# A cached-attention and ReGLU decode block: the last K loaded between two halves of a V, the last V but one as moving operand, and the W_o sets laid out anew

## The chip, the core and the metric

The kernel runs on one core of a Trainium2 chip. The core has a matrix engine (TensorE, PE in the profile; its weight loads are shown as PEld), a vector engine (VectorE, DVE), a scalar engine (ScalarE, ACT), GpSimd (POOL) and SyncE (SP), which here issues nearly all the transfers. The engines run on their own and wait for one another at semaphores. Sixteen DMA engines carry the data between the chip's memory (HBM) and the on-chip memory (SBUF); matmul results land in PSUM. The metric is the device time of one execution in microseconds (us), median of the runs; lower is better.

## The reference

Two sequences (B = 2), one new token each. Layer norm, attention over a cache of 8192 keys and values for 32 heads of width 128, output projection, residual; then layer norm, a gated MLP with a ReLU gate (F = 1376), residual. All tensors are bf16.

```python
D = 512; Hq = Hkv = 32; Sk = 8192; Dh = 128; F = 1376
q = (layernorm(x) @ wq)                       # per head
scores = einsum("bhqd,bhkd->bhqk", q, k_cache) * Dh ** -0.5
p = softmax(scores)
h = x + einsum("bhqk,bhkd->bhqd", p, v_cache) @ wo
n = layernorm(h)
gate = n @ W_gate; up = n @ W_up
out = h + (relu(gate) * up) @ W_down
```

K and V together are 268 MB of the 281 MB that are read: every key and every value is used once.

## The kernel before

**Steps.** One step handles one pair of heads of one sequence: N = 32 steps, numbered i = 0 to 31 (i // 16 is the sequence). K and V of a step are 4 MB each. `kbuf` and `vbuf` have two slots, used by i % 2. Each partition holds NT = 128 tokens of 128 numbers; partitions 0 to 63 belong to the one head, 64 to 127 to the other.

**Scores.** The work on K is shared. TensorE takes the last NPE = 32 of the 128 tokens of each partition (`scores_pe`, lines 287 to 330: 128x128 transposes at L311, ScalarE copies them out of PSUM at L313, a matmul with q at L302, small transposes back at L321). VectorE takes the first 96: `products` (L338) multiplies K in place by a replicated q, `scores` (L353, L357) adds up the 128 numbers of each token by halving. In the last step the split is 48 to 80 (`NPE_LAST`, `share`). `largest` (L368) spreads the maximum, `exponentials` (L380, L383) writes the weights to `pgz`, which also has two slots, and the sums to `zc`.

**Values.** `values(i, part)` (lines 390 to 415) holds 8 columns of `pgz` as stationary operand and streams V as the moving one: 32 matmuls of 512 columns, 16 in each half. ScalarE copies the result out (L406), and once per group of steps `o_ps` is picked from its diagonal blocks (L411, 8 small fp32 matmuls). `values_cols` (lines 417 to 426) turns this round: each 128x128 block of V is loaded as the stationary operand and multiplied by two columns, 128 weight loads and 128 matmuls, and the result needs no picking. The steps before the last two use `values`; i = 30 and i = 31 use `values_cols`.

**Output projection.** W_o is 4 MB. Where many rows of W_o are contiguous in HBM, several heads are treated as a set: `SETS` lists (first head, heads, partitions, place), `spread` (L437, L442) and `attend_set` (L456, L459, L461, L464) rearrange the head outputs to the layout that the set's rows have in SBUF. The heads from `HM` on are done one by one by `attend` (L472). A set is done when its heads are ready in the second sequence (`behind`).

**Order.** The program is written out by hand (`manual_schedule`): every engine runs its instructions in the order of the code. SP issues the loads in program order too, each when its buffer's last readers are done. The last loads are issued in this order: K 30 (584.2 us), V 29 (589.6), K 31 (604.1), V 30 (610.2), the four pieces of V 31 (623.3 to 630.2), W_gate, W_up and three pieces of W_down. W_gate and W_up go to slot 0 of `kbuf`, W_down to `wd_sb`. Up to eight transfers of this queue are on the way at once: each takes one of eight semaphores in turn.

**The end.** After the last step come the sums, `values_cols(31)`, the last heads' `attend`, the second layer norm (lines 541 to 552), gate and up (L561), and down (L588), whose last two chunks are those that are loaded last.

Of the kernel before, what the change touches and what calls it, by code (L numbers as in the profile page):

```python
# [7 lines left out]
ACT = mybir.ActivationFunctionType  # L8
# [15 lines left out]
def kernel(  # L24
# [13 lines left out]
    nc = tc.nc  # L38
# [5 lines left out]
    KC = D // P  # L44
# [6 lines left out]
    NPE = NT // 4  # L51
    NPE_LAST = 3 * NT // 8
    TPC = 8
# [12 lines left out]

    SETS = [(0, 16, P, 0), (16, 8, P, 16), (24, 3, 48, 32)]
    WO_T = 24
    HM = 27

    assert Sq == 1 and Hkv == Hq and Dh == P and D == KC * P and Hq == 32 and NPE % TPC == NPE_LAST % TPC == 0
    assert F == 11 * P - AGAIN
# [39 lines left out]

    QZ = 2 * NPE_LAST // 4
    qz = consts.tile([P, B, NG, 2 * QZ], bf16)
# [6 lines left out]

    def load_kv(cache, buf, i, pieces=1):
        b, g = steps[i]
        w = ROW // pieces
        for k in range(pieces):
            nc.sync.dma_start(
                out=buf[:, i % 2, k * w:(k + 1) * w],
                in_=_dram(cache, (b * Hkv + 2 * g) * Sk * Dh + k * w, [[ROW, P], [1, w]]),
            )
# [19 lines left out]
    with tc.manual_schedule():  # L149

        xr = wd_sb[0:B, 0, :]
        nc.scalar.dma_start(out=xr, in_=_dram(A_x, 0, [[D, B], [1, D]]))
# [19 lines left out]
        nc.gpsimd.memset(qz, 0.0)  # L172
        nc.gpsimd.memset(wbig[0:HALF, SETS[2][3] * D:(SETS[2][3] + SROWS[2]) * D], 0.0)
        nc.gpsimd.memset(placed, 0.0)
# [44 lines left out]

        for (h0, n, w, at), r in zip(SETS, SROWS):  # L220
            part, rows = (P, [[r * D, P]]) if w == P else (24, [[r * D, 6], [6 * r * D, 4]])
            for k in range(w // part):
                nc.sync.dma_start(
                    out=wbig[32 * k:32 * k + part, at * D:(at + r) * D],
                    in_=_dram(A_wo, (h0 * Dh + part * k * r) * D, rows + [[1, r * D]]),
                )
# [54 lines left out]

        def share(i):

            npe = NPE_LAST if i == N - 1 else NPE
            return NT - npe, npe

        def scores_pe(i):
            b, g = steps[i]
            s = i % 2
            kt = kbuf[:, s, :]  # L290
            nv, npe = share(i)


            U = npe // 4
# [12 lines left out]
            for c0 in range(0, npe, TPC):  # L307
                t_ps = ps2.tile([P, TPC, P], bf16, tag="tp")
                for k in range(TPC):
                    t = nv + c0 + k  # L310
                    nc.tensor.transpose(t_ps[:, k, :], kt[:, t * Dh:(t + 1) * Dh], ident)  # L311
                kTs[c0] = small.tile([P, TPC * P], bf16, tag="kT", name="kT", bufs=2)
                nc.scalar.activation(out=kTs[c0], in_=t_ps.rearrange("p t s -> p (t s)"), func=ACT.Copy)  # L313
                if c0:
                    times_q(c0 - TPC)
            times_q(npe - TPC)
# [7 lines left out]
            scol = small.tile([P, NT], f32, tag="scol")  # L324
            scols[i] = scol
            for j in range(2):
                r = slice(j * HALF, (j + 1) * HALF)
                nc.scalar.activation(  # L328
                    out=scol[r, nv:NT].rearrange("p (u t) -> p t u", t=4), in_=sc_ps[r, :, :, j], func=ACT.Copy,
                )  # L330

        def products(i):

            b, g = steps[i]
            kt = kbuf[:, i % 2, :]
            nv, _ = share(i)
# [7 lines left out]
        def scores(i):  # L344

            kt = kbuf[:, i % 2, :]
            scol = scols[i]
            nv, _ = share(i)
            width = Dh
# [40 lines left out]
        def values(i, part):  # L390
# [12 lines left out]
            if part == 0:  # L403
                return
            w = (g // 4) % 2
            nc.scalar.activation(out=pv[r, w], in_=pv_ps[i][r, :], func=ACT.Copy)  # L406
            if i in groups:
                first, n = groups[i][1:]
                o_ps[i] = ps.tile([P, 8], f32, tag="of", name="o_ps")
                for t in range(VG):  # L410
# [19 lines left out]
        def spread(k):  # L430

            h0, n, w, at = SETS[k]
            nq = Dh // SROWS[k]
            sps = []
            for b in range(B):
# [5 lines left out]
                if w != P:  # L441
                    nc.vector.tensor_copy(  # L442
                        _free(placed, b * HALF, [[32, 2], [1, 4], [4, 6]]), _free(sp, 0, [[24, 2], [6, 4], [1, 6]]),
                    )
                    sp = placed[:, b, :]
                sps.append(sp)
            return sps

        def attend_set(k, sps, last=False):

            h0, n, w, at = SETS[k]
            r = SROWS[k]
            p1 = P if w == P else HALF
            or_ps = ps.tile([P, B, r], f32, tag="mx")
            for b in range(B):
                nc.tensor.matmul(out=or_ps[0:p1, b, :], lhsT=sps[b], rhs=rest[k], start=True, stop=True)  # L456
            o, i = orow[k][0:p1], or_ps[0:p1].rearrange("p b c -> p c b")
            if last:
                nc.vector.tensor_copy(o, i)  # L459
            else:  # L460
                nc.scalar.activation(out=o, in_=i, func=ACT.Copy)  # L461
            for c0 in range(r):
                for c in range(KC):
                    nc.tensor.matmul(  # L464
                        out=att_ps[:, c, :],
                        lhsT=_free(wbig[0:p1], (at + c0) * D + c, [[KC, P]]), rhs=orow[k][0:p1, c0, :],
                        start=(k == 0 and c0 == 0 and c == 0), stop=False, skip_group_check=True,
# [21 lines left out]

        for i in range(N):  # L490
            last = i == N - 1
            if i >= 2:
                sums(i - 2)
            scores_pe(i)
            products(i)
            if i >= 2 and not last:
                for k, sps in behind(i - 2):
                    attend_set(k, sps)
            if last:
                values_cols(i - 1, 0, NT // 2)  # L500
            elif i >= 1:
                values(i - 1, 0)
            scores(i)
            largest(i)
            ready = behind(i - 2) if last else []
            exponentials(i)
            if last:
                values_cols(i - 1, NT // 2, NT)
                for k, sps in ready:
                    attend_set(k, sps, last=True)  # L510
            if i + 2 < N:
                load_kv(A_k_cache, kbuf, i + 2)
            if 1 <= i < N - 1:
                values(i - 1, 1)
            if i + 1 < N:
                load_kv(A_v_cache, vbuf, i + 1, pieces=4 if i + 1 == N - 1 else 1)
            if i == NG // 2:
                nc.sync.dma_start(out=wd_sb[:, FC - 1, :], in_=_dram(B_W_down, FSETS[-1][0] * D, [[D, P], [1, D]]))
            if i == N - 2:
                for w, src in ((0, B_W_gate), (1, B_W_up)):  # L520
                    nc.sync.dma_start(
                        out=wgu[:, w], in_=_dram(src, 0, [[KC * F, P], [F, KC], [1, F]]),
                    )
                for f0, n in FSETS[:-1]:
                    nc.sync.dma_start(
                        out=wd_sb[:, f0 // P:f0 // P + n, :],
                        in_=_dram(B_W_down, f0 * D, [[n * D, P], [1, n * D]]),
                    )
        sums(N - 2)
        shares(N - 2)  # L530
        normalise(N - 2)
        sums(N - 1)
        shares(N - 1)
        values_cols(N - 1)
        normalise(N - 1)
        for h in range(HM, Hq):
            attend(h)
# [87 lines left out]
```

## Time and profile before

The median of three runs is 664.61 us (664.50 to 664.61). The profiled execution took 664.74 us, with a span of 663.0 us from its first to its last instruction.

| what | value |
|---|---|
| profiled execution, span | 664.74 us, 663.0 us |
| HBM read | 281.09 MB, 424 GB/s over the span |
| queue of SP (q1) | 98.6% of 16 engines' span |
| PE, DVE, ACT, POOL busy | 74%, 72%, 33%, 3% |
| period of a step in the middle | 19.4 us (K issues 564.78 and 584.16 us) |
| last K issued, used from | 604.1 us, 629.4 us |
| last attend ends, y ends | 652.3 us, 659.2 us |

How to read it: "busy" is the time in which an engine executed, "idle before" the time just before a group of instructions and what ended it. The chain that ended last is followed back from the last instruction, at each point to what released it. The timeline gives each group of instructions with its start, its length and, in brackets, how long the engine had been idle. PEclk is the granted clock of TensorE, 1.0 being full speed. Besides the page, the trace holds one record for every packet that a DMA engine moved (start, length, bytes) and one for every increment of a semaphore.

### The profile page before, as it was taken

What the parts mean: (1) busy time and instruction counts of PE and PEld (TensorE: products, weight loads), DVE (VectorE), ACT (ScalarE), POOL (GpSimd) and SP (SyncE); (2) the same over time, 40 slices, a digit from 0 to 9 for tenths busy, and PEclk for the clock granted to TensorE, in tenths of its full rate; (3) what the DMA queues carried; (4) which work ended last, traced back from release to release, by engine and by line L of the source; (5) the groups of instructions that cost most, each with busy time, mean ns of one, the idle gap of its engine ahead of it and who ended that gap; (6) DMA issues with size and microseconds to landing.
All of it is one profiled execution on the core that took longest, in us unless ns stands there. A gap on an engine that the chain in (4) does not pass through costs nothing.

```text
span 663.0 us, 7717 instructions
## 1 busy us (share of the span) xinstructions
PE 489.4 (74%) x3282; PEld 229.2 (35%) x3282; DVE 475.9 (72%) x306; ACT 219.5 (33%) x400; POOL 17.8 (3%) x73
## 2 busy tenths in 40 slices
PE   3656777787777668787777867776877876788786
PEld 2422232333223333332333322333333432343266
DVE  0594788667778777778877767877777787776771
ACT  1532233333233333133333322333331333332250
POOL 8200000000000000000000000000000000000000
PEclk9968878988878998787899877899887888987785
DMA  9999999999999999999999999999999999999995
GB/s 380 431 413 445 424 443 428 427 439 430 429 436 437 426 441 427 427 440 431 430 435 428 434 433 432 429 434 437 426 435 438 422 435 438 431 432 432 433 417 202
DMA packets 11970, 281.58 MB, mean 425 GB/s; under 512 B 1518, under 2 KB 2288, under 8 KB 2672
## 3 DMA queue, kind: packets, MB, share of 16 engines
q1 hardware_dynamic: 11932, 281.09, 98.6%
q8 instruction: 25, 0.41, 0.2%
q14 instruction: 9, 0.07, 0.0%
q10 hardware_dynamic: 4, 0.00, 0.0%
HBM read 281.09 MB, written 0.00 MB: 424 GB/s over the span
## 4 chain that ended last, share of the span: by engine, by line
DMA 68%; PE 21%; DVE 9%; ACT 1%; issue 0%; SPq 0%; DVEq 0%; ACTq 0%
DMA vbuf<-in_A_v_cache_dram 53%; PE pv_ps L399 17%; DMA kbuf<-in_A_k_cache_dram 15%; DVE kbuf L353 4%; DVE kbuf L338 4%; PE o_ps L423 1%; PE mx_ps L368 1%; ACT kT L313 1%; DVE scol L357 1%; PE row_ps L302 0%; PE g_ps L561 0%; PE t_ps L311 0%; PE d_ps L588 0%; PE u_ps L561 0%; PE z_ps L268 0%
## 5 line engine op out<-in xcount | busy, mean ns | idle before, releaser
L399 PE MATMUL pv_ps<-vbuf,pgz 128*8 128x512 bf16 x960 | 277.6, 455 | 66.6 <-DMA vbuf<-in_A_v_cache_dram 66.6
L338 DVE TENSOR_TENSOR kbuf<-kbuf,qrep 128x12288 bf16<-128x12288 bf16 (+1 forms) x32 | 208.8, 6525 | 107.9 <-DMA kbuf<-in_A_k_cache_dram 107.9
L353 DVE TENSOR_TENSOR kbuf<-kbuf 128x6144 bf16<-128x6144 bf16 (+4 forms) x128 | 211.1, 1649 | 4.2
L399 PEld LDWEIGHTS <-pgz 128*8 128x8 bf16 x960 | 92.4, 99 | 227.8 <-issue 153.5
L313 ACT ACTIVATE kT<-t_ps 128x1024 bf16<-128x1024 bf16 x130 | 129.4, 1022 | 43.0 <-PE t_ps L311 40.9
L383 ACT ACTIVATE pgz<-scol,nm 64x128 bf16<-64x128 f32 x64 | 25.5, 399 | 263.0 <-DVE nm L380 262.2
L302 PE MATMUL row_ps<-kT,qz 128*16 128x512 bf16 (+1 forms) x260 | 78.5, 383 | 40.1 <-ACT kT L313 37.4
L311 PE MATMUL t_ps<-ident,kbuf 128*128 128x128 bf16 x1040 | 77.6, 225 | 10.6 <-DMA kbuf<-in_A_k_cache_dram 10.3
L311 PEld LDWEIGHTS <-kbuf 128*128 128x128 bf16 x1040 | 61.4, 101 | 51.1 <-issue 30.6
L302 PEld LDWEIGHTS <-qz 128*16 128x16 bf16 (+1 forms) x260 | 20.0, 87 | 63.2 <-issue 47.0
L406 ACT ACTIVATE pv<-pv_ps 8x512 f32<-8x512 f32 x30 | 17.6, 588 | 65.7 <-PE pv_ps L399 65.7
L380 DVE TENSOR_REDUCE nm<-mx_ps 128x2 f32<-128x128 f32 x32 | 9.3, 292 | 37.8 <-PE mx_ps L368 37.8
L357 DVE TENSOR_REDUCE scol<-kbuf 128x96 f32<-128x768 bf16 (+1 forms) x32 | 30.4, 949 | 1.1
L321 PE MATMUL sc_ps<-ident_f,rows 16*128 16x16 f32 (+1 forms) x128 | 13.4, 214 | 21.6 <-ACT rows L318 21.6
L318 ACT ACTIVATE rows<-row_ps 16x512 f32<-16x512 f32 (+1 forms) x32 | 18.8, 586 | 21.8 <-PE row_ps L302 21.8
L368 PE MATMUL mx_ps<-nscale,pm 128*128 128x128 f32 x64 | 16.2, 337 | 9.7 <-DVE pm L361 9.5
L321 PEld LDWEIGHTS sc_ps<-ident_f,rows 16*128 16x128 f32 (+1 forms) x128 | 10.3, 136 | 37.7 <-ACT rows L318 37.7
L328 ACT ACTIVATE scol<-sc_ps 64x32 f32<-64x32 f32 (+1 forms) x64 | 14.2, 223 | 17.0 <-PE sc_ps L321 16.2
L368 PEld LDWEIGHTS mx_ps<-nscale,pm 128*128 128x128 f32 x64 | 9.9, 195 | 23.4 <-DVE pm L361 16.0
L411 PE MATMUL o_ps<-pick,pv 128*128 128x8 f32 (+1 forms) x64 | 8.4, 258 | 5.5 <-ACT pv L406 5.5
L383 ACT ACTIVATION_READ_ACCUMULATOR pgz<-scol,nm 64x1 f32 x64 | 11.8, 185 | 0.0
L361 DVE TENSOR_REDUCE pm<-scol 128x1 f32<-128x128 f32 x32 | 9.2, 286 | 3.4 <-ACT scol L328 0.2
(91 smaller groups left out, 107.7 us busy)
## 6 DMA issues: line engine op xcount, KB each, us to landing
kbuf<-in_A_k_cache_dram SPq DMA_DIRECT2D x32, 4096.0 KB, 24.3
vbuf<-in_A_v_cache_dram SPq DMA_DIRECT2D x31, 4096.0 KB, 29.4
wbig<-in_A_wq_dram SPq DMA_DIRECT2D x1, 4096.0 KB, 12.1
vbuf<-in_A_v_cache_dram SPq DMA_DIRECT2D x4, 1024.0 KB, 18.2
wbig<-in_A_wo_dram SPq DMA_DIRECT2D x1, 2048.0 KB, 31.7
kbuf<-in_B_W_gate_dram SPq DMA_DIRECT2D x1, 1376.0 KB, 21.4
kbuf<-in_B_W_up_dram SPq DMA_DIRECT2D x1, 1376.0 KB, 24.2
wbig<-in_A_wo_dram SPq DMA_DIRECT2D x1, 1024.0 KB, 33.8
```

The costliest lines, as they stand in the source:

```text
L302: nc.tensor.matmul(out=row_ps, lhsT=qz[:, b, g, z0:z0 + 2 * U], rhs=kTs[c0][:, k * P:(k + 4) * P], start=(u == 0), stop=(u == U - 1),)
L311: nc.tensor.transpose(t_ps[:, k, :], kt[:, t * Dh:(t + 1) * Dh], ident)
L313: nc.scalar.activation(out=kTs[c0], in_=t_ps.rearrange("p t s -> p (t s)"), func=ACT.Copy)
L318: nc.scalar.activation(out=rows, in_=row_ps, func=ACT.Copy)
L321: nc.tensor.transpose(sc_ps[:, t].rearrange("p u j -> p (u j)"), rows[:, t * P:(t + 1) * P], ident_f[0:2 * U, 0:2 * U],)
L338: nc.vector.tensor_tensor(out=kv, in0=kv, in1=_free(qrep, (b * NG + g) * Dh, [[0, nv], [1, Dh]]), op=ALU.mult,)
L353: nc.vector.tensor_tensor(out=lo, in0=lo, in1=_free(kt, half, [[Dh, nv], [1, half]]), op=ALU.add,)
L357: nc.vector.tensor_reduce(out=scol[:, 0:nv], in_=_free(kt, 0, [[Dh, nv], [1, 8]]), axis=AXIS.X, op=ALU.add,)
L368: nc.tensor.matmul(out=mx_ps.rearrange("p a b -> p (a b)"), lhsT=_free(pms[i], 0, [[0, P]]), rhs=nscale, start=True, stop=True,)
L383: nc.scalar.activation(out=pgz[r, s, :, j, :], in_=scol[r, :].rearrange("p (u t) -> p u t", t=VG), func=ACT.Exp, scale=SCALE, bias=nm[r, j ...
L399: nc.tensor.matmul(out=pv_ps[i][r, :], lhsT=pgz[:, s, u].rearrange("p j t -> p (j t)"), rhs=vbuf[:, s, u * VG * Dh:(u + 1) * VG * Dh], sta ...
L406: nc.scalar.activation(out=pv[r, w], in_=pv_ps[i][r, :], func=ACT.Copy)
```

## The change

The three parts of the change:

1. **Loads.** V 29 is loaded in two halves: the first in step 28 as before, the second after K 31 in step 29. So K 31 stands in the queue before half of V 29. V 30 is loaded in two halves, V 31 in four pieces as before. `values(29, 1)` moves from step 30 to after `scores_pe(31)` and `products(31)`.
2. **Last two steps.** V 30 goes through `values` (moving operand, two halves, then `diagonals`, the former end of `values`) and no longer through `values_cols`. The split of the scores in the last step is 32 to 96 as in all the others. V 31 stays with `values_cols`, in four calls, between which the smaller work is placed. Step 31 is written out after the loop.
3. **W_o.** Sets before: 16 heads on 128 partitions, 8 on 128, 3 on 48, and five heads one by one. Sets after: 16 on 128, 4 on 32 (two transfers of 16 partitions of 16 KB, whose outer dimension in HBM is 4), 4 on 128 (kept in the part of `wd_sb` that W_down overwrites later), 4 on 128, and four heads one by one. The small set was read by two transfers of 24 partitions of 8 KB with an outer dimension of 6. GpSimd no longer clears a part of `wbig`.

```diff
-    SETS = [(0, 16, P, 0), (16, 8, P, 16), (24, 3, 48, 32)]
-    WO_T = 24
-    HM = 27
+    SETS = [(0, 16, P, 0), (16, 4, 32, 16), (20, 4, P, 0), (24, 4, P, 32)]
+    WO_T = 36
+    HM = Hq - 4
...
-    def load_kv(cache, buf, i, pieces=1):
+    def wo_set(k):
+        at = SETS[k][3] * D
+        return wd_sb.rearrange("p c n -> p (c n)")[:, at:] if k == 2 else wbig[:, at:]
+    def load_kv(cache, buf, i, pieces=1, which=None):
         b, g = steps[i]
         w = ROW // pieces
-        for k in range(pieces):
+        for k in range(pieces) if which is None else which:
...
-        xr = wd_sb[0:B, 0, :]
+        xr = wd_sb[0:B, FC - 2, :]
...
-        nc.gpsimd.memset(wbig[0:HALF, SETS[2][3] * D:(SETS[2][3] + SROWS[2]) * D], 0.0)
...
-        for (h0, n, w, at), r in zip(SETS, SROWS):
-            part, rows = (P, [[r * D, P]]) if w == P else (24, [[r * D, 6], [6 * r * D, 4]])
-            for k in range(w // part):
+        for k, ((h0, n, w, _), r) in enumerate(zip(SETS, SROWS)):
+            part, rows = (P, [[r * D, P]]) if w == P else (16, [[r * D, 4], [4 * r * D, 4]])
+            for j in range(w // part):
                 nc.sync.dma_start(
-                    out=wbig[32 * k:32 * k + part, at * D:(at + r) * D],
-                    in_=_dram(A_wo, (h0 * Dh + part * k * r) * D, rows + [[1, r * D]]),
+                    out=wo_set(k)[32 * j:32 * j + part, 0:r * D],
+                    in_=_dram(A_wo, (h0 * Dh + part * j * r) * D, rows + [[1, r * D]]),
                 )
...
-        def share(i):
-            npe = NPE_LAST if i == N - 1 else NPE
-            return NT - npe, npe
+        nv = NT - NPE
...
-            for c0 in range(0, npe, TPC):
+            for c0 in range(0, NPE, TPC):
...
-            w = (g // 4) % 2
-            nc.scalar.activation(out=pv[r, w], in_=pv_ps[i][r, :], func=ACT.Copy)
+            nc.scalar.activation(out=pv[r, (g // 4) % 2], in_=pv_ps[i][r, :], func=ACT.Copy)
+        def diagonals(i):
             if i in groups:
                 first, n = groups[i][1:]
+                w = (first // 4) % 2
...
                 if w != P:
                     nc.vector.tensor_copy(
-                        _free(placed, b * HALF, [[32, 2], [1, 4], [4, 6]]), _free(sp, 0, [[24, 2], [6, 4], [1, 6]]),
+                        _free(placed, b * HALF, [[32, 2], [1, 4], [4, 4]]), _free(sp, 0, [[16, 2], [4, 4], [1, 4]]),
                     )
-                    sp = placed[:, b, :]
+                    sp = placed[:, b, 0:48]
...
-        def attend_set(k, sps, last=False):
-            h0, n, w, at = SETS[k]
+        def attend_set(k, sps):
...
-            o, i = orow[k][0:p1], or_ps[0:p1].rearrange("p b c -> p c b")
-            if last:
-                nc.vector.tensor_copy(o, i)
-            else:
-                nc.scalar.activation(out=o, in_=i, func=ACT.Copy)
+            nc.scalar.activation(out=orow[k][0:p1], in_=or_ps[0:p1].rearrange("p b c -> p c b"), func=ACT.Copy)
...
-        for i in range(N):
-            last = i == N - 1
+        L = N - 1
+        for i in range(L):
             if i >= 2:
                 sums(i - 2)
             scores_pe(i)
             products(i)
-            if i >= 2 and not last:
-                for k, sps in behind(i - 2):
-                    attend_set(k, sps)
-            if last:
-                values_cols(i - 1, 0, NT // 2)
-            elif i >= 1:
+            ready = behind(i - 2) if i >= 2 else []
+            for k, sps in ready:
+                attend_set(k, sps)
+            if i >= 1:
                 values(i - 1, 0)
             scores(i)
             largest(i)
-            ready = behind(i - 2) if last else []
             exponentials(i)
-            if last:
-                values_cols(i - 1, NT // 2, NT)
-                for k, sps in ready:
-                    attend_set(k, sps, last=True)
             if i + 2 < N:
                 load_kv(A_k_cache, kbuf, i + 2)
-            if 1 <= i < N - 1:
+            if i == L - 2:
+                load_kv(A_v_cache, vbuf, i, 2, [1])
+            if 1 <= i < L - 1:
                 values(i - 1, 1)
-            if i + 1 < N:
-                load_kv(A_v_cache, vbuf, i + 1, pieces=4 if i + 1 == N - 1 else 1)
+                diagonals(i - 1)
+            if i + 1 < L:
+                load_kv(A_v_cache, vbuf, i + 1, 1 if i < L - 3 else 2, [0] if i == L - 3 else None)
             if i == NG // 2:
                 nc.sync.dma_start(out=wd_sb[:, FC - 1, :], in_=_dram(B_W_down, FSETS[-1][0] * D, [[D, P], [1, D]]))
-            if i == N - 2:
-                for w, src in ((0, B_W_gate), (1, B_W_up)):
-                    nc.sync.dma_start(
-                        out=wgu[:, w], in_=_dram(src, 0, [[KC * F, P], [F, KC], [1, F]]),
-                    )
-                for f0, n in FSETS[:-1]:
-                    nc.sync.dma_start(
-                        out=wd_sb[:, f0 // P:f0 // P + n, :],
-                        in_=_dram(B_W_down, f0 * D, [[n * D, P], [1, n * D]]),
-                    )
-        sums(N - 2)
-        shares(N - 2)
-        normalise(N - 2)
-        sums(N - 1)
-        shares(N - 1)
-        values_cols(N - 1)
-        normalise(N - 1)
-        for h in range(HM, Hq):
+        scores_pe(L)
+        products(L)
+        values(L - 2, 1)
+        diagonals(L - 2)
+        load_kv(A_v_cache, vbuf, L, pieces=4)
+        for w, src in ((0, B_W_gate), (1, B_W_up)):
+            nc.sync.dma_start(out=wgu[:, w], in_=_dram(src, 0, [[KC * F, P], [F, KC], [1, F]]))
+        for f0, n in FSETS[:-1]:
+            nc.sync.dma_start(
+                out=wd_sb[:, f0 // P:f0 // P + n, :], in_=_dram(B_W_down, f0 * D, [[n * D, P], [1, n * D]]),
+            )
+        values(L - 1, 0)
+        scores(L)
+        largest(L)
+        exponentials(L)
+        values(L - 1, 1)
+        sums(L - 2)
+        ready = behind(L - 2)
+        values_cols(L, 0, NT // 4)
+        diagonals(L - 1)
+        for k, sps in ready:
+            attend_set(k, sps)
+        sums(L - 1)
+        behind(L - 1)
+        values_cols(L, NT // 4, NT // 2)
+        sums(L)
+        shares(L)
+        for h in range(HM, HM + 2):
+            attend(h)
+        values_cols(L, NT // 2, NT)
+        normalise(L)
+        for h in range(HM + 2, Hq):
             attend(h)
```

More of the change, by code (lines that the diff above doesn't have):

```diff
@@ L51 @@
     NPE = NT // 4
-    NPE_LAST = 3 * NT // 8
     TPC = 8
@@ L63 @@
     AGAIN = 32
-    SETS = [(0, 16, P, 0), (16, 8, P, 16), (24, 3, 48, 32)]
-    WO_T = 24
-    HM = 27
-    assert Sq == 1 and Hkv == Hq and Dh == P and D == KC * P and Hq == 32 and NPE % TPC == NPE_LAST % TPC == 0
+    SETS = [(0, 16, P, 0), (16, 4, 32, 16), (20, 4, P, 0), (24, 4, P, 32)]
+    WO_T = 36
+    HM = Hq - 4
+    assert Sq == 1 and Hkv == Hq and Dh == P and D == KC * P and Hq == 32 and NPE % TPC == 0
     assert F == 11 * P - AGAIN
@@ L111 @@
     qT = consts.tile([P, B, Hq], bf16)
-    QZ = 2 * NPE_LAST // 4
+    QZ = 2 * NPE // 4
     qz = consts.tile([P, B, NG, 2 * QZ], bf16)
@@ L280 @@
         scols = {}
-        def share(i):
-            npe = NPE_LAST if i == N - 1 else NPE
-            return NT - npe, npe
+        nv = NT - NPE
+        U = NPE // 4
         def scores_pe(i):
             b, g = steps[i]
[L289 to L294, printed above, removed]
+            kt = kbuf[:, i % 2, :]
             row_ps = ps.tile([2 * U, 4 * P], f32, tag="row")
@@ L315, in scores_pe @@
                     times_q(c0 - TPC)
-            times_q(npe - TPC)
+            times_q(NPE - TPC)
             rows = small.tile([2 * U, 4 * P], f32, tag="rows", bufs=1)
@@ L323, in scores_pe @@
                 )
-            scol = small.tile([P, NT], f32, tag="scol")
-            scols[i] = scol
+            scols[i] = small.tile([P, NT], f32, tag="scol", name="scol")
             for j in range(2):
@@ L328, in scores_pe @@
                 nc.scalar.activation(
-                    out=scol[r, nv:NT].rearrange("p (u t) -> p t u", t=4), in_=sc_ps[r, :, :, j], func=ACT.Copy,
+                    out=scols[i][r, nv:NT].rearrange("p (u t) -> p t u", t=4), in_=sc_ps[r, :, :, j], func=ACT.Copy,
                 )
@@ L335, in products @@
             kt = kbuf[:, i % 2, :]
-            nv, _ = share(i)
             kv = _free(kt, 0, [[Dh, nv], [1, Dh]])
@@ L347, in scores @@
             scol = scols[i]
-            nv, _ = share(i)
             width = Dh
@@ L430, in spread @@
         def spread(k):
-            h0, n, w, at = SETS[k]
+            h0, n, w, _ = SETS[k]
             nq = Dh // SROWS[k]
@@ L442, in spread @@
                     nc.vector.tensor_copy(
-                        _free(placed, b * HALF, [[32, 2], [1, 4], [4, 6]]), _free(sp, 0, [[24, 2], [6, 4], [1, 6]]),
+                        _free(placed, b * HALF, [[32, 2], [1, 4], [4, 4]]), _free(sp, 0, [[16, 2], [4, 4], [1, 4]]),
                     )
-                    sp = placed[:, b, :]
+                    sp = placed[:, b, 0:48]
                 sps.append(sp)
             return sps
-        def attend_set(k, sps, last=False):
-            h0, n, w, at = SETS[k]
+        def attend_set(k, sps):
+            w = SETS[k][2]
             r = SROWS[k]
-            p1 = P if w == P else HALF
+            p1 = P if w == P else 48
             or_ps = ps.tile([P, B, r], f32, tag="mx")
@@ L465, in attend_set @@
                         out=att_ps[:, c, :],
-                        lhsT=_free(wbig[0:p1], (at + c0) * D + c, [[KC, P]]), rhs=orow[k][0:p1, c0, :],
+                        lhsT=_free(wo_set(k)[0:p1], c0 * D + c, [[KC, P]]), rhs=orow[k][0:p1, c0, :],
                         start=(k == 0 and c0 == 0 and c == 0), stop=False, skip_group_check=True,
```

## The prediction

> **What bounds the kernel now.** I read the page's DMA rows first, then the chain of waits, then the timeline of the end. The page:
>
> ```profile
> DMA  9999999999999999999999999999999999999995
> q1 hardware_dynamic: 11932, 281.09, 98.6%
> L399 PE MATMUL pv_ps<-vbuf,pgz 128*8 128x512 bf16 x960 | 277.6, 455 | 66.6 <-DMA vbuf<-in_A_v_cache_dram 66.6
> ```
>
> The sixteen DMA engines are full from start to end, and TensorE waits for V. So up to about 640 us no work on an engine matters as long as loads are issued in time; the change moves no bytes away. What it can win or lose lies in how long the slowest DMA engine takes, and in what follows the last data. The chain of waits over the end:
>
> ```profile
> 630.87 1.05 PE o_ps L411 x8
> ...
> 641.14 1.70 PE o_ps L423 x64
> 642.84 0.64 PE mx_ps L368 x2
> 643.48 1.68 PE o_ps L423 x64
> 645.16 0.21 PE or_ps L456 x2
> ...
> 645.61 1.20 PE att_ps L464 x32
> 646.81 0.53 PE z_ps L268 x2
> ...
> 648.24 3.41 PE o_ps L423 x128
> 651.65 0.68 PE att_ps L472 x20
> ...
> 657.46 1.50 PE d_ps L588 x44
> ...
> 658.98 0.17 DVE y L593
> ```
>
> From 631 us the chain is TensorE in program order: it is a queue of work, not a wait. The attention ends at 652.33; from there to y at 659.15 are 6.82 us of norm and MLP, which the change leaves alone.
>
> The DMA side is close behind. The trace's packet records fall into sixteen streams (a 32 KB packet every 1.21 us, 0.038 us per KB). No stream ever runs dry, but they end apart: three at 651.1 to 651.3 us, most at 654 to 656, the last at 658.1. What sets them back shows in the records. Every instruction fetch for TensorE (16 KB) costs one stream about 1.42 us, in turn over eight streams; fetches for other engines (8 KB) cost 0.55 to 0.84 us, always on the same streams. The small W_o set (two transfers, six increments of the semaphore each instead of sixteen) costs six streams 2.46 us each. The last stream has both: it is one of the six and takes three TensorE fetches, 7.03 us behind the first. Behind it come 5.14 and 4.75, also of the six, with three and four small fetches. The last W_down piece thus lands at about 658.4, and y could not come before 658.9: the slack of the data against the chain is 0.2 to 0.3 us.
>
> **The change, part by part.**
>
> *W_o.* Bytes per stream: before 232 KB, 296 on the six; after 224, 352 on the four. Worked at 0.038 us per KB: the four lose 2.13 us, the two let go win 2.74, the other ten win 0.30. If the four are among the six and do not hold the last stream (three TensorE fetches), that one ends 2.7 us earlier, and the new last is 5.14 + 2.13 = 7.27 or 4.75 + 2.13 = 6.88 behind, against 7.03: the data ends 0.15 us earlier to 0.24 later. If they do hold it, 2.13 later. The trace doesn't show which; two bounds therefore, and I take the first: of the six only one lies in the ring of eight, so if both are rows of neighbours it sits at an end of the six; and four of the other five carry the other engines' fetches, none of which falls outside, so the row seems to begin there.
>
> The Trainium skill, "DMA: Bandwidth & Descriptors", section "Why a DMA increments its semaphore by 16 and not by 1", says that a transfer uses the lowest-numbered k engines, k dividing the outermost sizes; no run here shows numbers. The same page's "Rules for kernel authors" speaks against the edit: an outermost size below 16 confines the transfer to that many engines. By the rule alone 512 KB on four would put the end 2.1 us later; by the streams above it falls mostly on engines with room.
>
> In step 29 the sets grow from 32 to 80 matmuls: 48 x 0.0375 (1.20 us for 32) = 1.8 us, plus a second round of L456 and its copy, 0.2 + 0.6, so 2.6 us on TensorE, and on VectorE two more spreads and two copies, 0.8 us. Cover: K 31 is then issued near 604.9 instead of 604.1 and must be there when the fastest stream has finished half of V 29, near 607; V 30's second half near 613.6, needed at 626. Without that cover the streams would idle; the slow ones have 4 to 7 us more. `values(28, 0)` starts at 602.7 instead of 600.1, and at half clock (6.8 us) ends at 609.5; the maximum and VectorE's nm then end at 610.4, 0.35 us after K 30 has landed, so VectorE's step 30 shifts by 0.35. GpSimd loses a 3.5 us clear and gets about 40 more selects of 0.25 us, 10 us, ending near 29 us; first needed in step 25. W_o comes in six transfers instead of five: with eight on the way at most, the heads' one waits for K 0 (24.1 us) and V 1 for V 0 (43.4 instead of 41.2 us); K 2 and W_o fill the streams till about 60. The heads one by one: 16 instead of 20 matmuls of 0.034, -0.14 us, counted below.
>
> *Loads.* K 31 lands half a V earlier: 629.37 - 4.85 = 624.5. SP issues two transfers more (0.33 each); V 31's last pieces wait for `values(29, 1)`, so they go out at 634 to 637.5 instead of 628.5 and 630.2. Behind them on SP stand W_gate, W_up and W_down. The fastest streams need the third piece at 636: at worst they idle 2 us of their 7 us of slack. Cost nothing.
>
> *Last two steps.* The sum on TensorE, full clock: step 30's scores run 613.6 to 620.4 (6.82, as 610.08 to 616.90), `values(29, 0)` to 624.0, then it waits for VectorE: 610.4 + 6.56 + 6.73 + 0.95 + 0.3 = 625.05, maximum to 625.5. From there without a gap:
>
> - scores of step 31: 6.82
> - three half V's of 3.56: `values(29, 1)`, both of V 30: 10.68
> - copy of pv and the two picks (0.68 + 1.05 + 1.05): 2.78
> - mx 0.45, three sums z (0.4, 0.55, 0.5): 1.90
> - 128 weight loads of V 31: 3.50
> - last W_o set: 0.2 + 0.3 + 0.6: 1.10
> - last normalise 0.3, four heads 0.66: 0.96
>
> Together 27.7, attention ends at 653.25 against 652.33: +0.9. VectorE's step 31 (625.95 + 6.56 + 6.73 + 1.25 = 640.5) and the weights' exponentials are ready before the line reaches them (mx at 641), V 31 has landed at 648.7 before its last half is due at 650.9. V 30 as moving operand costs 7.1 us where weight loads cost 3.4.
>
> *The clock.* The timeline shows what half clock costs:
>
> ```profile
> 619.73 6.50 PE L399 MATMUL pv_ps<-vbuf,pgz 128*8 128x512 bf16 x16 [2.83 <-DMA vbuf<-in_A_v_cache_dram]
> 626.58 3.62 PE L399 MATMUL pv_ps<-vbuf,pgz 128*8 128x512 bf16 x16
> ```
>
> A half V is 6.50 cold, 3.6 warm; scores_pe 8.07 (at 24.17 us) and 9.15 (at 39.56) against 6.82. The granted clock changes on a grid of 3.41 us. Of the stretches at full clock in which PE was busy under 60%, 25 of 27 were followed by half clock; from 60 to 66%, 5 of 9; above, 1 of 94. The 1.1 us of idleness before 625 and the thin end of scores_pe give stretches of 62 to 66%: even chances. So the price is between 0 and 2.3 us; I take 0.6, half of the milder row. Likeliest: +0.9 + 0.6 = +1.5 us, with bounds +0.6 (sum 0.3 too dear) and +3.2.
>
> The skill's page "TensorE: Matmul & The Clock Gate", "Part 1: The HAM clock gate", says the clock drops after an idle window of about 3.4 us. By that the 1.1 us would cost nothing, and the sum would be +0.9; the rows here drop at far less idleness, and they decide.
>
> **Sum.** 664.74 in the profiled execution (span 663.0 and 1.7 around it) + 1.5 = 666.2; the median shown is 0.13 lower: 666.1.
>
> **Rivals.**
>
> 1. *The four engines hold the last stream.* For: it is one of six. Against: the ring argument above. Data ends at 660.5, y at 661.2: +2.0, 666.6, if TensorE is earlier; else the larger of the two.
> 2. *No change: TensorE is done when the data is.* Place: the moving halves of V 30. They run while TensorE would wait, if mx, copies and picks overlap with them. Price: y is bounded by the data, -0.2 to +0.5: 664.7. It decides if the sum of 27.7 is 0.9 too long. For: K 31 is there 4.9 us sooner, and step 31 spares 2.3 us of scores (9.1 to 6.8). Against: one engine, in order, at every row's own price.
> 3. *Faster: the four lie on streams without other load.* Then the last is about 4.9 behind, data ends 2.2 us earlier; with rival 2's TensorE, -1.6: 663.0. Against: it needs both.
>
> **How the numbers follow.** Chances: likeliest 0.58, rival 1 0.14, rival 2 0.22, rival 3 0.06. 0.2% is 1.33 us, about what a measurement can tell from no change. The likeliest lies above +1.33 in about two thirds of its cases, 0.40, and with rival 1 slower is 0.54; same 0.18 + 0.22 = 0.40; faster 0.06. The likeliest's own range is 665.2 to 667.8. The range of 664.4 to 667.8 takes in rival 2's lower bound and leaves out rival 3 and the cold ends.
>
> **What would show it.** In the timeline: K 31 used from about 625.5; 32 matmuls of 512 columns for V 30, 0.22 us each where warm, between 637 and 647; only 128 weight loads of V, those of V 31; the chain of the end still TensorE without a wait for DMA; attention's end near 654. Packet records: the last stream among the four, about 7 us behind. Wrong if the chain ends in a wait for W_down (rival 1), or TensorE waits for V 31 (rival 2), or if K 31's earlier issue lets a stream run dry.

## The result and the profile after

The changed kernel takes 665.69 us (median of 19 runs, 664.69 to 666.97); the kernel before takes 664.61 us (19 runs beside them, 664.14 to 666.23). The ratio is 1.0015, 95% interval 1.0008 to 1.0022: 1.1 us slower, at the edge of what can be told from no change. The forecast was 666.1 us with a range of 664.4 to 667.8. The profiled execution took 666.97 us (span 665.2), the longest of the 19, so its end lies about 1.3 us later than in a usual run. Three executions among all that are reported here lie far off (698.77, 751.71 and 1020.20 us) and are left out of every ratio and range.

The page of the changed kernel, rows as shown of before and one that is new:

```profile
DMA  9999999999999999999999999999999999999994
...
q1 hardware_dynamic: 12216, 281.09, 98.4%
...
L394 PE MATMUL pv_ps<-vbuf,pgz 128*8 128x512 bf16 x992 | 275.8, 441 | 60.8 <-DMA vbuf<-in_A_v_cache_dram 60.8
...
L237 POOL TENSOR_SCALAR_AFFINE_SELECT rest<-rest 128x4 bf16<-128x4 bf16 (+1 forms) x80 | 36.8, 460 | 5.5
```

The bytes are the same and the DMA engines are still full until the end. `values` has 32 matmuls more, those of V 30. The last row is GpSimd's selects. Its mean of 460 ns mixes two lengths: the first 48 take about 0.26 us each, as put in, and the last 32, from 20.2 to 49.8 us, 0.93 us each. GpSimd works 45.7 us in all and is done near 53 us instead of 29; none of the steps waits for it. The chain of waits of the changed kernel, from the last maximum but one to y (start, length, what):

```profile
624.62 0.50 PE mx_ps L363 x2
...
625.52 0.50 ACT pgz L378 x2
...
626.04 0.49 ACT pgz L378 x2
...
626.55 1.03 ACT kT L311
627.59 0.04 issue
627.63 1.01 PE row_ps L300 x2
...
634.36 0.42 PE sc_ps L319 x4
634.77 3.56 PE pv_ps L394 x16
...
639.00 1.06 PE o_ps L409 x8
640.05 3.55 PE pv_ps L394 x16
643.60 0.42 PE mx_ps L363 x2
644.02 3.55 PE pv_ps L394 x16
...
652.38 1.72 PE o_ps L421 x64
...
654.34 0.41 PE att_ps L466 x8
...
659.30 1.49 PE d_ps L595 x44
...
660.81 0.17 DVE y L600
```

The order of the row is the predicted one: three half V's of 3.55 us, 32 moving matmuls for V 30, weight loads only for V 31, no transfer in the chain. It ends at 654.75 where before's ended at 652.33. It is clearly longer than predicted in one place: from 624.94, where the scores of step 31 begin, to 634.77 are 9.83 us; 6.82 were put in for them.

The data end close behind. The sixteen increments of the last W_down piece but one (us; from the trace's semaphore records):

```
before  650.8 651.0 651.0 653.3 653.7 653.8 655.0 655.1 655.2 655.2 655.3 655.3 655.3 655.5 655.9 657.8
after   653.2 653.3 653.3 653.4 653.5 654.8 654.8 654.9 655.0 655.1 655.1 655.2 655.4 656.4 657.7 658.1
```

The last stream of the changed kernel is one of the four that carry the small W_o set, 7.05 us behind the first by its packets when V 30 and V 31 are loaded. At the end it is 4.9 behind, because the fastest streams waited about 2 us for V 31's last pieces, at no cost. Both are as predicted, though these pieces were issued at 636.6 and 638.4 us, later than put in. But the slack was counted from the wrong piece. Behind the last piece (658.7) lie 8 matmuls of d_ps; behind the piece before it lie 28, 1.10 us. In the kernel before this piece lands at 657.81, and 657.81 + 0.05 + 1.10 + 0.02 (the steps of run 3's chain below) is 658.98, just where y starts. So before stood on two limits at once, with no slack, and in the changed kernel the limit of the data, too, rises by 0.3 (658.10 in the profile above) to 0.4 us (658.21 in run 3).

### The profile page after: what moved, and what is told of

Read it like the earlier page. It is cut to its first block, busy times and chain, and to the rows that moved or that the text cites. A ratio compares the mean times of both kernels' runs of the same rounds, so it can differ in the third digit from the quotient of the medians.

```text
span 665.2 us, 7649 instructions
## 1 busy us (share of the span) xinstructions
PE 488.5 (73%) x3204; PEld 228.7 (34%) x3204; DVE 478.2 (72%) x307; ACT 218.5 (33%) x401; POOL 45.7 (7%) x116
## 4 chain that ended last, share of the span: by engine, by line
DMA 59%; DVE 34%; PE 5%; ACT 1%; issue 1%; SPq 0%; DVEq 0%; ACTq 0%
DMA kbuf<-in_A_k_cache_dram 59%; DVE kbuf L348 16%; DVE kbuf L334 16%; DVE scol L352 2%; PE pv_ps L394 2%; PE o_ps L421 1%; PE row_ps L300 0%; ACT kT L311 0%; PE o_ps L409 0%; PE t_ps L309 0%; PE d_ps L595 0%; PE g_ps L568 0%; PE u_ps L568 0%; PE z_ps L271 0%; ACT pgz L378 0%
## 5 line engine op out<-in xcount | busy, mean ns | idle before, releaser
L334 DVE TENSOR_TENSOR kbuf<-kbuf,qrep 128x12288 bf16<-128x12288 bf16 x32 | 209.9, 6558 | 106.5 <-DMA kbuf<-in_A_k_cache_dram 106.5
L348 DVE TENSOR_TENSOR kbuf<-kbuf 128x6144 bf16<-128x6144 bf16 (+3 forms) x128 | 212.1, 1657 | 4.2
L300 PE MATMUL row_ps<-kT,qz 128*16 128x512 bf16 x256 | 80.2, 396 | 40.1 <-ACT kT L311 37.7
L300 PEld LDWEIGHTS <-qz 128*16 128x16 bf16 x256 | 19.6, 88 | 64.1 <-issue 49.1
L237 POOL TENSOR_SCALAR_AFFINE_SELECT rest<-rest 128x4 bf16<-128x4 bf16 (+1 forms) x80 | 36.8, 460 | 5.5
L352 DVE TENSOR_REDUCE scol<-kbuf 128x96 f32<-128x768 bf16 x32 | 30.5, 953 | 1.1
L319 PE MATMUL sc_ps<-ident_f,rows 16*128 16x16 f32 x128 | 13.3, 213 | 21.6 <-ACT rows L316 21.6
L316 ACT ACTIVATE rows<-row_ps 16x512 f32<-16x512 f32 x32 | 18.8, 587 | 22.1 <-PE row_ps L300 22.1
L319 PEld LDWEIGHTS sc_ps<-ident_f,rows 16*128 16x128 f32 x128 | 10.2, 136 | 38.1 <-ACT rows L316 38.1
L325 ACT ACTIVATE scol<-sc_ps 64x32 f32<-64x32 f32 x64 | 14.3, 223 | 17.0 <-PE sc_ps L319 16.2
```

The lines of the kernel that those rows point to most:

```text
L237: nc.gpsimd.affine_select(out=re, in_=re, compare_op=ALU.not_equal, fill=1.0, base=-k * r, pattern=[[-1, r]], channel_multiplier=1,)
L300: nc.tensor.matmul(out=row_ps, lhsT=qz[:, b, g, z0:z0 + 2 * U], rhs=kTs[c0][:, k * P:(k + 4) * P], start=(u == 0), stop=(u == U - 1),)
L319: nc.tensor.transpose(sc_ps[:, t].rearrange("p u j -> p (u j)"), rows[:, t * P:(t + 1) * P], ident_f[0:2 * U, 0:2 * U],)
L334: nc.vector.tensor_tensor(out=kv, in0=kv, in1=_free(qrep, (b * NG + g) * Dh, [[0, nv], [1, Dh]]), op=ALU.mult,)
L348: nc.vector.tensor_tensor(out=lo, in0=lo, in1=_free(kt, half, [[Dh, nv], [1, half]]), op=ALU.add,)
L352: nc.vector.tensor_reduce(out=scol[:, 0:nv], in_=_free(kt, 0, [[Dh, nv], [1, 8]]), axis=AXIS.X, op=ALU.add,)
```

## The experiments

The theory on record was that TensorE's row sets the end; the main rival, that the slowest DMA streams do. The first four kernels take the change apart. The kernel before took 664.75 us beside them, 664.81 beside the next four, 664.77 beside runs 9, 11 and 12 and 664.63 beside run 10.

**1. Only the new W_o sets.** The kernel before with the changed sets, loads and spread:

```diff
-    SETS = [(0, 16, P, 0), (16, 8, P, 16), (24, 3, 48, 32)]
+    SETS = [(0, 16, P, 0), (16, 4, 32, 16), (20, 4, P, 0), (24, 4, P, 32)]
...
```

> The kernel before with the new W_o sets alone. Theory (TensorE's queue sets the new kernel's end, and the W_o sets shift load among the DMA streams without moving the last one): the data ends within 0.3 us of before; TensorE's tail is 0.7 us shorter (16 matmuls of the last set instead of 32, 16 of single heads instead of 20), but y is held by the last W_down piece. 664.2 to 664.9 us, no change. Rival (the 1.1 us of the whole change come from the W_o sets: from the 80 matmuls in step 29 or from the later data): 665.3 or more.

Measured: 665.42 us, ratio 1.0009 (1.0000 to 1.0017): a miss, 0.7 us slower instead of about the same. Its chain of waits:

```profile
647.21 3.41 PE o_ps L426 x128
650.62 0.13 PE att_ps L475 x4
650.75 1.95 issue
652.70 0.55 PE att_ps L475 x12
...
657.80 1.49 PE d_ps L591 x44
...
659.31 0.17 DVE y L596
```

TensorE stands still for 1.95 us in the middle of the heads, waiting for nothing that the profile shows; a 16 KB instruction fetch for it began at 650.49. Yet it hardly costs anything: the last W_down piece but one lands at 658.10 here, and 658.10 + 1.17 is 659.27, 0.04 us before y's start. Without the stop the data would have held y as well, as in runs 3 and 4 below.

**2. Only the order.** The changed kernel with the old W_o sets and loads.

> The new kernel with the old W_o sets, so the loads and the last two steps alone. Theory: without the 48 extra matmuls in step 29, TensorE is through values(29, 0) near 620.6 and idles 3.9 us until the maximum of step 30, so the clock is at half during the scores of step 31 in every run, and the last set has 32 matmuls instead of 16: 666.4 to 667.6 us, with little spread. Rival (the clock does not matter): 665.3 to 666.0 with the same two clusters as the new kernel. Rival (W_o costs the time): as before, 664.6.

Measured: 666.86 us, ratio 1.0034 (1.0022 to 1.0046): the predicted row alone costs 2.1 us, as expected. The six runs spread from 665.94 to 668.79, though. Its chain, between the halves of V 31:

```profile
648.36 1.19 PE att_ps L459 x32
...
653.58 0.36 PE att_ps L467 x7
653.94 0.44 issue
654.39 0.21 PE att_ps L467
```

With the old sets the last set in the row is the one on 48 partitions, 32 matmuls; in the changed kernel it is 16 matmuls, 0.67 us. So the two parts don't add (0.7 + 2.1 against 1.1): the new sets make the data later and shorten TensorE's row by 0.5 us.

**3. V 30 stationary again,** in the otherwise changed kernel:

```diff
-        values(L - 1, 0)
+        values_cols(L - 1, 0, NT // 2)
...
-        values(L - 1, 1)
+        values_cols(L - 1, NT // 2, NT)
...
-        diagonals(L - 1)
```

> The new kernel with V 30 back as stationary operand (two times 64 weight loads at the same places, no picking for step 30). Theory: TensorE's queue loses 3.7 us of matmuls and 1.05 us of picking, the attention ends when V 31 has landed (near 651.6), and y is held by the last data: 664.5 to 665.1 us, the two clusters gone. Rival (the data ends later in the new kernel and sets its time): no change against it, 665.3 to 666.9.

Measured: 665.36 us, ratio 1.0007 (0.9999 to 1.0016), above the expectation. TensorE's row is now shorter by 3.7 us, and the time hardly falls. The end of its chain:

```profile
639.69 18.52 DMA wd_sb<-in_B_W_down_dram
658.21 0.05 issue
658.25 1.10 PE d_ps L594 x28
659.36 0.02 issue
659.38 0.17 DVE y L599
```

This is the data's limit by itself, 0.6 us above the kernel before, with the 28 matmuls behind the late piece.

**4. TensorE kept busy ahead of step 31's scores.** Eight matmuls of 512 columns, their result unread, before the maximum of step 30:

```diff
             scores(i)
+            if i == L - 1:
+                fill = ps.tile([P, VG * Dh], f32, tag="row", name="fill")
+                for u in range(8):
+                    nc.tensor.matmul(
+                        out=fill[0:2 * VG, :], lhsT=pgz[:, 1, u].rearrange("p j t -> p (j t)"),
+                        rhs=vbuf[:, 1, u * VG * Dh:(u + 1) * VG * Dh], start=(u == 0), stop=(u == 7),
+                    )
             largest(i)
```

> The new kernel with 8 matmuls of 512 columns, whose result nobody reads, in the 2 us in which TensorE waits for the maximum of step 30. Theory: the two clusters of the new kernel's times (664.7 to 665.9 and 666.7 to 667.0) are the clock at full and at half during the scores of step 31; kept busy, all runs are at 664.9 to 665.7 and none at 666.5 or more. Rival (the clusters come from elsewhere, such as the DMA streams): both clusters stay.

Measured: 665.72 us, ratio 1.0016 (1.0007 to 1.0024), one run of eleven at 667.19: no gain at the median, and the spread did not vanish. Runs above 666.5 us are 1 of 11 here and 6 of 19 in the changed kernel, too few to tell apart. The granted clock changes on a grid of 3.41 us, which lies elsewhere in each execution. Busy times by stretch in the changed kernel, whose grid has edges at 623.28, 626.70 and 630.11 (the first number after the length is PE's busy time; behind POOL stand the granted clock, the DMA share and GB/s):

```profile
623.00:626.70 3.70, 1.38 (x18) 1.28 (x19) 2.98 (x5) 1.13 (x5) 0.00 (x0) 1.00 0.99 421
626.70:630.10 3.40, 2.47 (x12) 0.96 (x11) 3.40 (x1) 2.19 (x3) 0.00 (x0) 0.50 1.02 431
630.10:633.50 3.40, 3.18 (x14) 1.10 (x12) 3.37 (x2) 1.65 (x2) 0.00 (x0) 0.50 1.00 426
```

and with the fillers, on the grid of that execution:

```profile
621.67:625.09 3.42, 2.70 (x21) 1.20 (x19) 2.69 (x4) 0.00 (x0) 0.00 (x0) 1.00 0.93 393
625.09:628.50 3.41, 1.77 (x25) 1.25 (x23) 3.38 (x2) 2.92 (x6) 0.00 (x0) 1.00 1.03 440
628.50:631.91 3.41, 2.52 (x19) 0.98 (x16) 3.38 (x2) 2.32 (x3) 0.00 (x0) 1.00 1.03 435
```

In the changed kernel TensorE is busy 1.38 us of the grid stretch before 626.70, 40%, and half clock follows. With the fillers the stretch that holds the wait is 79% busy and the clock stays at 1.00, even behind the next one, which is 52% busy. The scores, from 624.91 to sc_ps's end at 632.70, take 7.79 us instead of 9.83, so the half clock costs TensorE 2.04 us. But the chain then ends in the transfer of W_down (landed 658.24, y at 659.42), as in run 3. Only the longest run of the changed kernel was traced: which clock a usual one has is not shown. The Trainium skill, "TensorE: Matmul & The Clock Gate", section "Part 1: The HAM clock gate", asks for an idle window of about 3.4 us; here a stretch that was 40% busy was followed by half clock.

**5, 6, 7. W_o evenly over all streams.** One set of 8 and one of 4 heads on 128 partitions in place of the sets of few partitions, so that no load is confined to fewer DMA engines: in the kernel before, in run 3's kernel and in the changed one.

```diff
+    SETS = [(0, 16, P, 0), (16, 8, P, 16), (24, 4, P, 24)]
+    WO_T = 28
+    HM = Hq - 4
...
```

The kernel before with it:

> The kernel before with W_o evenly over all streams: sets of 16, 8 and 4 heads on 128 partitions and four single heads, no set on a part of the partitions. Theory: every stream carries 256 KB of W_o, the one that was last loses 1.5 us, the three-fetch streams gain 0.9, the last ones are then 5.5 us behind instead of 7.0: the last-but-one W_down piece lands 1.5 us earlier and no longer holds y. TensorE's queue of the old order, 0.7 us shorter, sets the end: 663.8 to 664.5 us. Rival (the lag of the streams does not reach the end): 664.6 to 665.4, as with the new sets alone.

Run 3's kernel with it:

> The new kernel with the even W_o and V 30 as stationary operand. Theory: neither bound is left where it was; W_down lands 1.5 us earlier, TensorE is through with the attention near 650.5, 1.8 us earlier than before, and y follows the data: 662.9 to 663.5 us, little spread. Rival (another bound, such as the landing of V 31 or code fetches, stands just behind): 664.2 or more.

The changed kernel with it:

> The new kernel with the even W_o and nothing else. Theory: the data ends 1.5 us earlier, but TensorE's queue with V 30 as moving operand sets the end; without the 48 extra matmuls in step 29 the clock is at half in the scores of step 31, as with the old sets: 665.8 to 667.2 us. Rival (the data sets the end of the new kernel): 663.8 to 664.5.

| kernel | us | range | ratio to before |
|---|---|---|---|
| before, even sets | 664.51 | 663.22 to 665.07 | 0.9992 (0.9983 to 1.0001) |
| V 30 stationary, even sets | 663.64 | 663.31 to 664.34 | 0.9982 (0.9973 to 0.9992) |
| changed, even sets | 665.24 | 664.12 to 665.63 | 1.0004 (0.9995 to 1.0013) |

Against what was expected, the first lies at the upper bound, the second 0.14 us above it and the third 0.6 below the lower one. The middle one beats both kernels: 1.2 us under before, 1.7 under run 3, which differs from it in the W_o sets alone. Its end:

```profile
638.37 18.02 DMA wd_sb<-in_B_W_down_dram
656.39 0.04 issue
656.43 1.11 PE d_ps L594 x28
657.55 0.02 issue
657.57 0.17 DVE y L599
```

The same piece lands 1.8 us earlier than in run 3, and y comes 1.8 us earlier. The streams lie closer together: from the first to the last increment of K 30 it is 4.6 us, and 7.3 in run 3. With V 30 moving, the same data bring nothing more: the chain is TensorE again, y at 659.52.

```profile
653.08 0.41 PE att_ps L466 x8
...
658.02 1.48 PE d_ps L595 x44
659.50 0.02 issue
659.52 0.17 DVE y L600
```

So V 30 as moving operand costs 1.6 us where the data don't hide it (665.24 against 663.64), and the four engines cost 1.7 us where TensorE doesn't hide them (665.36 against 663.64). By these medians the changed kernel has both at similar height and pays about once. The expectation for the last of the three was too high by 0.6 us, for a reason worth seeing. VectorE's last step but one, from which TensorE's row starts, waits for K 30. In the changed kernel:

```profile
609.85 6.56 DVE L334 TENSOR_TENSOR kbuf<-kbuf,qrep 128x12288 bf16<-128x12288 bf16 x1 [0.82 <-DMA kbuf<-in_A_k_cache_dram]
```

and with even sets:

```profile
608.50 6.56 DVE L334 TENSOR_TENSOR kbuf<-kbuf,qrep 128x12288 bf16<-128x12288 bf16 x1 [3.10 <-DMA kbuf<-in_A_k_cache_dram]
```

K 30 is there when the slowest stream has brought its part (last increment at 609.8 and 608.5). A late stream thus delays the start of TensorE's row as well as the end of the data.

In the kernel before, the even sets gain only 0.3 us. In its profile all streams but one have the last W_down piece by 657.0; the sixteenth increment comes at 658.15, after a TensorE instruction fetch that ran from 655.85 to 656.78. That this fetch delayed it was not tested.

**8. More on the four.** The changed kernel with the small set loaded a second time, into partitions that nothing reads.

```diff
+        for j in (2, 3):
+            nc.sync.dma_start(
+                out=wbig[32 * j:32 * j + 16, 16 * D:32 * D],
+                in_=_dram(A_wo, (16 * Dh + 256 * (j - 2)) * D, [[16 * D, 4], [64 * D, 4], [1, 16 * D]]),
+            )
```

> The new kernel with the small W_o set loaded a second time, into partitions that nobody reads: 128 KB more on each of the four streams. Theory: no stream ever runs dry, so the 4.85 us of these bytes, moved in the first 60 us, are still there at the end: 669.8 to 670.6 us. Rival (the lag is caught up on the way, or hidden): less than half of it, 665.5 to 667.9.

Measured: 676.01 us, ratio 1.0173 (1.0159 to 1.0188): 10.3 us above the changed kernel, twice what the bytes make. The packet records say how: while the extra transfers ran, 54 to 64 us, the packets of every stream took about twice their time (32 KB 2.0 to 2.6 us instead of 1.21, 16 KB 1.25 instead of 0.61).

**9, 10. One more transfer on the four,** into sixteen partitions beside the small set, in run 3's kernel; once from the rows of W_o just read, once from rows of W_down that nobody else reads then.

```diff
+        nc.sync.dma_start(
+            out=wbig[16:32, 16 * D:32 * D],
+            in_=_dram(A_wo, 16 * Dh * D, [[16 * D, 4], [64 * D, 4], [1, 16 * D]]),
+        )
```

> The run with the last-but-one V stationary, and one more transfer of 256 KB on four DMA engines into sixteen partitions beside the small set (what it brings is multiplied by zeros). 64 KB for each of the four at 0.038 us per KB is 2.43 us. Theory (the four hold the last stream): 665.36 + 2.43 = 667.8, range 667.3 to 668.3, packets at their usual 1.21 us for 32 KB. Rival (as in the run that loaded the set twice, all packets take twice as long while the extra transfer is under way): about 1.5 to 3 us more, 669.3 to 670.8. If the four did not hold the end: 665.4 to 666.5.

> As the run with one more transfer of 256 KB on four DMA engines, with the same place in memory, the same form and the same size, but the transfer reads rows of W_down, which nothing else reads until the end, where that run read rows of W_o that had just been read for the small set (what it brings is multiplied by zeros). Theory (reading the same rows twice within some us halves the rate of all sixteen streams): packets of 32 KB stay at 1.21 us, and only the four's own 64 KB count, 365.36 + 300 = 665.36 + 2.43 = 667.8, range 667.3 to 668.3. Rival (the place or form of the write halves the rate): 670.0 to 670.8, with packets of about 2.5 us between 53 and 58 us, as there.

Measured: 670.41 us (two runs; 1.0085, 1.0064 to 1.0107) and 670.23 us (three runs; 1.0078, 1.0053 to 1.0104); the "365.36 + 300" on record is a slip for 665.36. The rival holds both times: the source doesn't matter. The stretch in which the third transfer runs, with the source in W_down:

```profile
53.00:58.00 5.00, 3.35 (x16) 1.52 (x17) 1.74 (x4) 0.98 (x4) 0.00 (x0) 1.00 0.96 224
```

and the same stretch of the changed kernel:

```profile
53.00:58.00 5.00, 3.44 (x17) 1.52 (x18) 1.65 (x4) 0.98 (x4) 0.00 (x0) 1.00 1.00 428
```

Half the rate for 5 us. On each of the four the extra transfer is four packets of 1.25 us, 5.0 us instead of the 2.43 that its bytes take at the usual rate. A stream outside the four loses half of 5 us, 2.5. The kernels lost 5.0 and 4.9 us against run 3: the whole of what the four lost. That shows, at two doses (10.3 for two transfers), that the four hold the end. The increments say the same: the last four of sixteen stand apart, and for K 30 the last comes 9.4 to 9.6 us behind the first instead of the 7.3 of run 3. What halves the rate is not settled: two transfers of this form into partitions 0 to 15 and 32 to 47 don't do it, a third into 16 to 31, or into 64 to 79 and a fourth into 96 to 111, do.

**11, 12. The same small set over sixteen engines.** The rows one after the other, so that the loads are no longer confined to four; shapes and work unchanged. First with V 30 stationary, then in the changed kernel.

```diff
-            part, rows = (P, [[r * D, P]]) if w == P else (16, [[r * D, 4], [4 * r * D, 4]])
+            part, rows = (P, [[r * D, P]]) if w == P else (16, [[r * D, 16]])
...
-                        _free(placed, b * HALF, [[32, 2], [1, 4], [4, 4]]), _free(sp, 0, [[16, 2], [4, 4], [1, 4]]),
+                        _free(placed, b * HALF, [[32, 2], [1, 16]]), _free(sp, 0, [[16, 2], [1, 16]]),
```

> The changed kernel with the last-but-one V stationary, as in the run that was bound by the data (665.36, last W_down piece but one at 658.2, y at 659.38), and the small W_o set laid out row after row, so that its two transfers can spread over sixteen DMA engines instead of four. TensorE's work and every set's shape are the same. Theory (the four engines set the end): each of the sixteen carries 32 KB of the small set, the four lose 96 KB, 3.6 us; the end falls to that of the even layout, 663.4 to 664.0, with y near 657.6 and every stream within about 4.6 us of the first. Rival (the step's longer work or the place of W_o beside W_down costs the time, not the four engines): 665.1 to 665.6.

> The changed kernel complete, with the same edit alone: the small W_o set over sixteen DMA engines. Theory: the data then ends near 656.5 and only TensorE's row of work sets the end, as in the even layout with the last-but-one V moving (665.24); 664.6 to 665.4, and the chain over the end holds no transfer. Rival (data and TensorE together set no more than TensorE alone does): 665.5 to 665.9.

Measured: 671.38 us (1.0094, 1.0076 to 1.0112), and 667.9 to 669.8 us for the changed kernel (1.0063, 1.0045 to 1.0081). Theory and rival both fall: instead of gaining 1.7 us the edit loses 6.0. The stretches of the first:

```profile
40.00:45.00 5.00, 4.18 (x27) 2.34 (x25) 5.00 (x2) 3.46 (x7) 4.86 (x3) 0.50 0.99 421
45.00:50.00 5.00, 4.11 (x22) 1.84 (x22) 4.97 (x2) 2.54 (x5) 4.93 (x3) 0.76 1.07 193
50.00:55.00 5.00, 2.81 (x14) 1.02 (x13) 4.57 (x6) 0.00 (x0) 1.86 (x2) 1.00 0.94 197
```

While the sixteen engines write into two groups of sixteen partitions, the rate is below half for 10 us, with 16 KB packets of up to 2.8 us instead of 0.61. So these two runs say nothing on the confinement by itself. The nearest comparison remains run 3 against the even sets, in which the shapes of the sets and their work in step 29 differ too; runs 8 to 10 are what ties the end to the four.

## Why the prediction was right, and where not

- **That TensorE in program order sets the end** was half of it. For the longest run it holds, and run 2 shows the row's price at 2.1 us. But by the medians the changed kernel stands on two limits: with TensorE's row shortened it takes 665.36, with the data made earlier 665.24, with both 663.64. That the forecast came within 0.4 us of the median is partly luck: in the profile the row ends 0.9 us later than put in even with the 0.6 for the clock, and a usual run ends 1.3 us before the profiled one.
- **The sum of 27.7 us from 625.5.** In the profile the row runs from 624.94 to 654.75. It starts 0.6 us earlier than put in, step 31's scores take 3.0 us more, the rest 0.9 less: 653.25 - 0.6 + 3.0 - 0.9 = 654.75. The term "scores of step 31: 6.82" is the one that failed, by two causes: 2.04 us are the half clock, and the other 0.97, which run 4 has too (7.79), are the wait for the first `kT`. TensorE waits 2.07 us for the maximum and 1.63 for this copy, because ScalarE has two exponentials (`pgz`, 625.52 to 626.53) ahead of it. The prediction counted 1.1 us of idleness, and for the first `kT` the 0.66 of the step before.

```profile
624.62 0.49 PE L363 MATMUL mx_ps<-nscale,pm 128*128 128x128 f32 x2 [2.07 <-DVE pm L356]
627.63 1.01 PE L300 MATMUL row_ps<-kT,qz 128*16 128x512 bf16 x2 [1.63 <-ACT kT L311]
```

- **The clock, 0.6 us at even chances.** The rule from the trace mostly held: in the changed kernel's trace 25 of 28 stretches under 60% busy were followed by half clock. It is no sharp line: the stretch of 52% in run 4 was not, nor was one of 48% in run 3. What was mis-sized is the busy share, 40% instead of 62 to 66%. Half clock came there, for one to three stretches, in every profile of the new order that was looked at without fillers (the changed kernel, runs 2, 3, 6 and 7). Its price in the profile is 2.0 us, near the upper bound of 2.3; the medians with and without fillers, 665.72 and 665.69, show none of it.
- **Step 29 grows by 2.6 us, VectorE's step 30 shifts by 0.35.** The work grew by 2.2 us (from the sets' start at 599.08 to 603.20, before 598.14 to 600.10). The shift didn't come: `values(28, 0)` ended at 608.3 and not at 609.5, and K 30 came last anyway.
- **W_o, the data 0.15 us earlier to 0.24 later.** The four indeed lie outside those that held the last stream, and the new last is 7.05 us behind (6.88 to 7.27 were put in, counted from where the first stream ended before). The piece landed 0.3 to 0.4 us later all the same, and the slack, "0.2 to 0.3 us", was nil, since the piece with 28 matmuls behind it was overlooked. By runs 1 and 3 this part costs 0.6 us.
- **Rival 1, four engines hold the last stream.** It was rightly rejected in the form given: from one transfer to the next the last four increments slip by at most 0.87 us (changed kernel, 80 to 610 us), never by the 1.42 us of a TensorE fetch. But the four become the last by their bytes, and the limit of the data that the rival describes is there in runs 3 and 4: 0.6 us above before in run 3's median, not 2.0.
- **Rival 2, no change.** Its statement, TensorE is done when the data is, fits the medians; only the data's end was not where before's was.
- **A rule weighed.** The Trainium skill's page "DMA: Bandwidth & Descriptors", section "Rules for kernel authors", spoke against an outermost size under 16. That agrees with 1.7 us between run 3 and the even sets. But giving the same two groups of sixteen partitions sixteen engines cost 6 us: here only the layout on 128 partitions gained, and more engines alone did not.

## What to carry to other kernels

When sixteen DMA streams never run dry, ask of every load how many of them it uses: what it adds to the slowest stream is paid at the end, and at every earlier wait for a whole tile. Find the data's limit by counting the work that stands behind each of the last pieces, not only behind the very last. Before an engine's row is shortened or lengthened, measure both limits apart, for where they lie within half a microsecond only an edit that lowers both gains anything.

## What the runs showed of the hardware

- Transfers of 256 KB into sixteen partitions can halve the rate of all DMA traffic while they run (193 to 243 GB/s instead of 410 to 450), with the engines shown as busy throughout. Two of them on four engines each did not, a third did, and two on sixteen engines did.
- A granted clock of one half followed a stretch of 3.41 us with TensorE busy 40%; in run 4 full clock stayed after stretches of 79% and 52%. The price of half clock was 2.04 us over one step's scores.
- TensorE stopped for 0.4 to 1.95 us in rows of short matmuls without a wait that the profile shows (the kernel before and runs 1 and 2). Each time it went on 1.28 to 1.35 us after the packet of an instruction fetch had ended; that the fetch is the cause was not tested.
- Why single runs of the changed kernel spread over 2.3 us, and those of run 3 over 0.3 us in their spans, stays open. With the fillers one run of eleven was still at 667.19.
